# A fourth column buffer, paced prefetches and held loads around the down projection of a transformer-block training step

## The chip, the cores and the metric

The kernel runs on one core of one Trainium2 chip. The metric is the device time of one execution in microseconds (us); lower is better. A time quoted for a kernel is the median of its runs. Runs of one kernel spread by 0.4 to 0.8%, so every comparison is made by ratio against the kernel before, run in the same rounds on the same chip, with a 95% interval.

## The reference

The program computes a pre-layernorm block, linear attention followed by a SwiGLU feed-forward net, and then all its gradients. S = 2048 tokens, D = 640, F = 1728, 32 heads, bfloat16.

```python
h  = x + attention(layernorm(x), wqkv, wo)          # linear attention, phi = elu+1
h2 = h + (silu(n @ w_gate) * (n @ w_up)) @ w_down   # n = layernorm(h)
return h2, and the gradients of x, wqkv, wo, w_gate, w_up, w_down for grad_out
```

## The kernel before

The token axis is cut into ST = 16 tiles of 128 rows. The parts that matter come in this order:

- Phase A builds a mask `Mbd` (which elements belong to the same head) by small matmuls, and uses it in phase A and again in phase D.
- The feed-forward stage makes m, dg and du (features by tokens) and stores them in device memory. Its last matmuls are `accw` (weight gradients), whose results are stored from `dw_sb`.
- The down projection (`accf`) reads one column block `mcols` of m per tile. Between its tiles the gate and up weights are transposed on TensorE (`pt_w`).
- The dh1 stage (`acch`) reads `dgcols` and `ducols` per tile. During it, three big tensors for phase D (`oTr`, `rdenTr`, `pqTr`) are prefetched in 12 pieces of 640 KB.

A scheduler places each engine's instructions. Program order is its guide, not its result, so loads may be issued earlier than the text of the kernel suggests.

```python
    Mbd = const.tile([P, DT, D], BF16, name="Mbd")      # held for the whole kernel
# ... phase A
        for i in range(DT):
            for (n0, n1) in NCH:
                ps = psA.tile([P, 512], FP32, name="ps_mbd", tag="mm")
                nc.tensor.matmul(ps[:, :n1 - n0], lhsT=Efull[:, i * P:(i + 1) * P], rhs=Efull[:, n0:n1], start=True, stop=True)
                nc.vector.tensor_copy(out=Mbd[:, i, n0:n1], in_=ps[:, :n1 - n0])
# ... after the feed-forward stage (whose dw_sb, dwd_sb buffers come from a pool "dwo", bufs=2)
            wgT = wTp.tile([P, FT, D], BF16, name="wgT")
            wuT = wTp.tile([P, FT, D], BF16, name="wuT")
            if fsz[-1] < P:
                nc.any.memset(wgT[fsz[-1]:, FT - 1, :], 0.0)
                nc.any.memset(wuT[fsz[-1]:, FT - 1, :], 0.0)
            stream4 = pb4.enter_context(tc.tile_pool(name="stream4", bufs=3))
            stream = pwd.enter_context(tc.tile_pool(name="stream", bufs=3))
            # ...
            def load_cols(t):
                dgcols = stream4.tile([P, FT, P], BF16, name="dgcols")
                ducols = stream4.tile([P, FT, P], BF16, name="ducols")
                for (cols, scr_vv, eng) in ((dgcols, scr_dgT_v, nc.sync), (ducols, scr_duT_v, nc.scalar)):
                    eng.dma_start(out=cols[:, :, :], in_=scr_vv[:, :, t * P:(t + 1) * P])
                return dgcols, ducols
            # ... down projection
            for t in range(ST):
                if t == ST - 1:
                    for te in range(min(2, ST)):
                        early_cols[te] = load_cols(te)
                mcols = stream.tile([P, FT, P], BF16, name="mcols")
                nc.sync.dma_start(out=mcols[:, :, :], in_=scr_mT_v[:, :, t * P:(t + 1) * P])
                # ... 2 x 14 matmuls accf, h2t = accf + h1, store h2t
                if t < len(wblocks):
                    weight_rowblock_T(*wblocks[t], t)        # 14 transposes pt_w
            # ... dh1 stage
            for t in range(ST):
                for (dst_ap, src_ap) in pf_at.get(t, []):    # one of 12 pieces per tile, by the program's text
                    nc.gpsimd.dma_start(out=dst_ap, in_=src_ap)
                # ... dgcols, ducols = early or load_cols(t); 2 x 28 matmuls acch
                ln_bwd_tile(accs, hn_tm[:, t, :], rstd2[:, t:t + 1], dh2_tm[:, t, :], dh1_tm[:, t, :], workL)
```

## Time and profile before

The time is 1116.3 us (1113.9 to 1118.1, five runs). The profiled execution spans 1117.2 us.

| what | us | where to read it |
|---|---|---|
| TensorE busy | 1056.8 (95%) | busy table of the page |
| TensorE waits for the fourth tile's dgcols | 11.2 | waits of PE |
| TensorE waits for the first mcols | 4.1 | waits of PE |
| last accw matmul issued to first accf | 7.1 | timeline (607.75 to 614.86) |
| dh1 stage, first to last acch | 135.2 | timeline (687.12 to 822.36) |

The first view is the list of TensorE's waits in the kernel before: who waited, for whom, then microseconds in total, number of times, longest. Lines are left out at each `...`; the largest entry of all, 13.6 us for `xn_tm` (10.9 of it before TensorE's first matmul), is among them, and the change does not touch it.

```profile
...
PE acch L663 <- DMA dgcols<-scr_dgT: 11.2, 1, 11.2
PE accf L621 <- DMA mcols<-scr_mT: 4.1, 1, 4.1
PE pt_tr L127 <- ACT o_tm L91: 3.7, 3, 2.8
...
PE accw L561 <- ACT dw_sb L91: 2.9, 1, 2.9
...
PE ps_mbd L323 <- DVE Mbd L324: 1.0, 3, 0.4
...
```

The second view is the chain that ended last in the kernel before, in order of time: start, length, what the chain went through.

```profile
608.13 6.69 DMA mcols<-scr_mT
614.86 14.19 PE accf L621 x84
...
687.12 5.88 PE acch L663 x42
693.02 28.23 DMA dgcols<-scr_dgT
721.30 101.37 PE acch L663 x728
```

A load whose median is 3.9 us took 28.2 us. The timeline of POOL, the engine that issues the prefetch, suggests why (start, length, engine, line, what, and in brackets the idle time before it):

```profile
690.42 3.48 POOL L651 DMA_DIRECT2D oTr<-scr_oT  x4 [2.52 <-issue]
693.90 3.43 POOL L651 DMA_DIRECT2D rdenTr<-scr_rdenT  x4
697.32 1.72 POOL L651 DMA_DIRECT2D pqTr<-scr_pqT  x2
699.88 0.86 POOL L651 DMA_DIRECT2D pqTr<-scr_pqT  x1 [0.85 <-DMA oTr<-scr_oT]
702.14 0.87 POOL L651 DMA_DIRECT2D pqTr<-scr_pqT  x1 [1.40 <-DMA oTr<-scr_oT]
```

The text asks for one piece per tile, but nothing holds a piece back. All 12, 7.9 MB, are issued within 12 us. The view by stretches of time gives busy time of each engine, the granted TensorE clock, the DMA share and GB/s for the dh1 stage of the kernel before:

```profile
core 0: us, PE busy (x) PEld busy (x) DVE busy (x) ACT busy (x) POOL busy (x), PEclk, DMA share, GB/s
686.00:695.00 9.00, 8.42 (x63) 5.93 (x62) 0.49 (x1) 0.71 (x3) 5.12 (x7) 1.00 0.38 115
695.00:720.00 25.00, 15.10 (x112) 10.66 (x109) 7.11 (x19) 4.11 (x12) 5.76 (x7) 0.85 1.07 325
720.00:730.00 10.00, 8.70 (x48) 5.55 (x49) 1.77 (x2) 1.35 (x3) 0.00 (x0) 0.70 1.04 166
730.00:822.00 92.00, 92.00 (x680) 66.28 (x678) 35.53 (x84) 22.62 (x60) 0.00 (x0) 1.00 0.45 101
```

The DMA engines are full from 695 to 720, TensorE loses about 10 of those 25 us, and the granted clock is low afterwards (0.70 in 720 to 730). From 730 on, with the prefetch over, TensorE is never idle.

### The profile page before, as it was taken

Reading aid. Unit: us, or ns where it says so; the run is one execution under the profiler, and the core shown is the slowest. Engines: PE = TensorE matmul, PEld = TensorE weight load, DVE = VectorE, ACT = ScalarE, POOL = GpSimd, SP = SyncE. Lnnn points to the kernel's source line nnn. Section 1 sums busy time; section 2 is a strip of 40 time slices with the busy share of each in tenths; the row PEclk is TensorE's granted clock in tenths of the full one; section 3 lists DMA queues with packets and bytes.
Section 4 is the critical chain, followed back from the end, with each engine's and each line's share of the span. In section 5 each row is a group of like instructions: output and inputs, shape, how many; then the busy total and the mean of one; then the engine's idle time right before and its main releaser. Section 6 shows DMA issues by size and latency. Waiting matters only on the chain.

```text
span 1117.2 us, 20344 instructions
## 1 busy us (share of the span) xinstructions
PE 1056.8 (95%) x8297; PEld 716.7 (64%) x8337; DVE 572.1 (51%) x1441; ACT 483.4 (43%) x951; POOL 133.8 (12%) x224
## 2 busy tenths in 40 slices
PE   5899998999999999999997999599989999899998
PEld 2477664575847576666756677377767467577775
DVE  8766676727273545545361232234343985477321
ACT  6755586526262535345351010122233686744231
POOL 2100000120202111111312013000000000011110
PEclk9899898999999999999999899799999999999999
DMA  8234364312222222212045954955440039411100
GB/s 318 81 132 161 147 248 145 124 62 86 92 82 95 78 102 78 97 45 104 31 165 175 219 127 143 299 116 127 100 152 32 1 115 358 177 42 43 42 36 31
DMA packets 134669, 134.24 MB, mean 120 GB/s; under 512 B 92384, under 2 KB 115680, under 8 KB 134320
## 3 DMA queue, kind: packets, MB, share of 16 engines
q0 software_dynamic: 20208, 77.58, 18.7%
q1 hardware_dynamic: 85440, 48.03, 15.3%
q10 hardware_dynamic: 28928, 7.34, 3.3%
q8 instruction: 65, 1.06, 0.4%
q14 instruction: 28, 0.23, 0.1%
HBM read 71.50 MB, written 61.42 MB: 119 GB/s over the span
## 4 chain that ended last, share of the span: by engine, by line
PE 78%; DVE 8%; DMA 7%; ACT 5%; issue 2%; POOLq 0%; POOL 0%; ACTq 0%; DVEq 0%; SPq 0%
PE accw L561 10%; PE acch L663 10%; PE acc_dxn L837 6%; PE accf L621 6%; PE acc_dwqkv L856 6%; PE pu L498 5%; PE pg L494 4%; PE acc L552 4%; PE pt_trs L127 4%; PE pt_tr L127 4%; PE pdm L502 3%; DMA dgcols<-scr_dgT 3%; PE ps_k L336 2%; PE acc_dwo L697 2%; PE ps_v L341 2%; PE ps_do L721 2%
## 5 line engine op out<-in xcount | busy, mean ns | idle before, releaser
L561 PEld LDWEIGHTS <-hn_tm 128*128 128x128 bf16 x1120 | 108.6, 99 | 15.4 <-issue 4.0
L663 PE MATMUL acch<-wgT,dgcols 128*128 128x320 bf16 x448 | 67.9, 304 | 11.8 <-DMA dgcols<-scr_dgT 11.2
L494 PE MATMUL pg<-hnT,wg_blk 128*128 128x512 bf16 (+1 forms) x266 | 72.7, 383 | 4.0 <-DMA wg_blk<-in_B_w_gate_dram 3.4
L498 PE MATMUL pu<-hnT,wu_blk 128*128 128x512 bf16 (+1 forms) x274 | 74.5, 384 | 0.4
L89 DVE CAST dw_sb<-accw 128x256 bf16<-128x256 f32 (+1 forms) x35 | 14.5, 415 | 112.5 <-PE accw L561 81.8
L502 PE MATMUL pdm<-dh2T,wdT 128*128 128x512 bf16 (+1 forms) x274 | 69.3, 379 | 1.4 <-ACT dm L511 1.0
L552 PE MATMUL acc<-dh_tm,m_strip 128*128 128x320 bf16 (+1 forms) x448 | 69.3, 299 | 0.0
L621 PE MATMUL accf<-wd_big,mcols 128*128 128x320 bf16 x448 | 65.0, 307 | 4.1 <-DMA mcols<-scr_mT 4.1
L663 PE MATMUL acch<-wuT,ducols 128*128 128x320 bf16 x448 | 66.6, 300 | 0.0
L856 PE MATMUL acc_dwqkv<-cur_tm,xn_tmr 128*128 128x320 bf16 x480 | 65.7, 299 | 0.0
L561 PE MATMUL accw<-dg_strip,hn_tm 128*128 128x256 bf16 (+1 forms) x560 | 62.0, 273 | 2.9 <-ACT dw_sb L91 2.9
L663 PEld LDWEIGHTS <-dgcols 128*128 128x128 bf16 x448 | 44.4, 99 | 30.1 <-DMA dgcols<-scr_dgT 11.5
L561 PE MATMUL accw<-du_strip,hn_tm 128*128 128x256 bf16 (+1 forms) x560 | 60.3, 269 | 0.6 <-DVE dw_sb L89 0.6
L621 PEld LDWEIGHTS <-mcols 128*128 128x128 bf16 x448 | 44.1, 100 | 22.6 <-DMA mcols<-scr_mT 4.2
L856 PEld LDWEIGHTS <-xn_tmr 128*128 128x128 bf16 x480 | 46.9, 98 | 18.1
L91 ACT CAST dw_sb<-accw 128x256 bf16<-128x256 f32 (+1 forms) x35 | 12.8, 365 | 104.6 <-PE accw L561 102.0
L214 ACT ACTIVATE lb_dy<-acch 128x320 bf16<-128x320 f32 x32 | 14.0, 437 | 98.1 <-PE acch L663 98.1
L663 PEld LDWEIGHTS <-ducols 128*128 128x128 bf16 x448 | 44.1, 98 | 17.5
L552 PEld LDWEIGHTS <-m_strip 128*128 128x128 bf16 (+1 forms) x448 | 41.8, 99 | 13.6 <-issue 0.3
L502 PEld LDWEIGHTS <-wdT 128*128 128x128 bf16 (+1 forms) x280 | 27.0, 98 | 34.5 <-DVE wdT L89 3.1
L229 DVE SCALAR_TENSOR_TENSOR lb_t<-lb_dy,lb_nm,lb_t 128x640 bf16<-128x640 bf16 x32 | 28.2, 881 | 40.6 <-ACT lb_t L227 40.6
L565 POOL DMA_DIRECT2D out_dram<-dw_sb x70 | 37.9, 541 | 80.2 <-DVE dw_sb L89 45.2
(264 smaller groups left out, 2066.9 us busy)
## 6 DMA issues: line engine op xcount, KB each, us to landing
scr_mT<-mT_row POOLq DMA_DIRECT2D x14, 512.0 KB, 3.0
scr_duT<-duT_row POOLq DMA_DIRECT2D x14, 512.0 KB, 3.7
scr_dgT<-dgT_row POOLq DMA_DIRECT2D x14, 512.0 KB, 2.9
ducols<-scr_duT ACTq DMA_DIRECT2D x16, 448.0 KB, 4.6
mcols<-scr_mT SPq DMA_DIRECT2D x16, 448.0 KB, 4.1
dgcols<-scr_dgT SPq DMA_DIRECT2D x16, 448.0 KB, 3.9
out_dram<-dw_sb POOLq DMA_DIRECT2D x60, 64.0 KB, 1.8
x_tm<-in_A_x_dram SPq DMA_DIRECT2D x4, 640.0 KB, 6.2
```

The lines of the kernel that those rows point to most:

```text
L127: nc.tensor.transpose(out=pt[:cols_in, j * rows_in:(j + 1) * rows_in], in_=src, identity=ident[:rows_in, :rows_in])
L229: nc.vector.scalar_tensor_tensor(out=t2[:], in0=dy[:], scalar=nm[:, 0:1], in1=t1[:], op0=ALU.subtract, op1=ALU.subtract)
L494: nc.tensor.matmul(pg[:fs, :], lhsT=wg_blk[:, kt, coff:coff + fs], rhs=hnT[:, kt, cs], start=(kt == 0), stop=(kt == DT - 1))
L498: nc.tensor.matmul(pu[:fs, :], lhsT=wu_blk[:, kt, coff:coff + fs], rhs=hnT[:, kt, cs], start=(kt == 0), stop=(kt == DT - 1))
L502: nc.tensor.matmul(pdm[:fs, :], lhsT=wdT_i[:, kt, :], rhs=dh2T[:, kt, cs], start=(kt == 0), stop=(kt == DT - 1))
L552: nc.tensor.matmul(acc[:fs, :w], lhsT=m_strip[:, t, coff:coff + fs], rhs=dh2_tm[:, t, n0:n1], start=(t == 0), stop=(t == ST - 1))
L561: nc.tensor.matmul(acc[:, :gw], lhsT=hn_tm[:, t, dt_ * P:(dt_ + 1) * P], rhs=strip[:, t, :gw], start=(t == 0), stop=(t == ST - 1))
L565: nc.gpsimd.dma_start(out=o_ap[dt_ * P:(dt_ + 1) * P, gcol0:gcol0 + gw], in_=dw_sb[:, :gw])
L621: nc.tensor.matmul(acc[:, :w], lhsT=mcols[:, j, :], rhs=wd_nat[:, j, n0:n1], start=(j == 0), stop=(j == FT - 1))
L663: nc.tensor.matmul(acc[:, :w], lhsT=cols[:, j, :], rhs=wT[:, j, n0:n1], start=(k == 0), stop=(k == 2 * FT - 1))
L837: nc.tensor.matmul(acc[:, :w], lhsT=srcT[:, jj, t * P:(t + 1) * P], rhs=wqkvT[:, j, n0:n1], start=(k == 0), stop=(k == D3T - 1))
L856: nc.tensor.matmul(acc[:, :w], lhsT=xn_tmr[:, t, dt_ * P:(dt_ + 1) * P], rhs=cur_tm[:, t, n0:n1], start=(t == 0), stop=(t == ST - 1))
```

## The change

The intent is to remove both waits. `Mbd` no longer stays in the scratchpad for the whole kernel: it is built twice, which frees room for a fourth pair of column buffers. Each prefetch piece waits for the end of the tile before. The first four pairs of column loads wait until the down projection has started on the tile of the same number, so that the first mcols has no company. The first three mcols wait for the last accw matmul. The tile loops are also split into pairs (TB = 2). In the program's text this moves the first two pairs of column loads from before the last tile of the down projection to before the last two, and the change also puts each tile's column loads ahead of its prefetch piece.

```diff
-    Mbd = const.tile([P, DT, D], BF16, name="Mbd")
+    def build_mbd(Mbd_t, ps_pool, tag):
+        ...                                             # the same matmuls, evictions on either engine:
+                nc.any.tensor_copy(out=Mbd_t[:, i, n0:n1], in_=ps[:, :n1 - n0])
...
+        Mbd = kvA.tile([P, DT, D], BF16, name="Mbd")    # phase A
+        build_mbd(Mbd, psA, "mm")
...
-            stream4 = pb4.enter_context(tc.tile_pool(name="stream4", bufs=3))
+            stream4 = pb4.enter_context(tc.tile_pool(name="stream4", bufs=4))
...
-                    eng.dma_start(out=cols[:, :, :], in_=scr_vv[:, :, t * P:(t + 1) * P])
+                    d = eng.dma_start(out=cols[:, :, :], in_=scr_vv[:, :, tp * P:(tp + 1) * P])
+                    if tp < 4:
+                        tc.add_manual_dep(d.ins, down_mm[tp].name, SYNC, reason="first mcols tile goes alone")
...
+                    if t < 3:
+                        tc.add_manual_dep(dm_.ins, last_w.ins.name, SYNC, reason="not beside the dw_sb stores")
...
+                        d = nc.gpsimd.dma_start(out=dst_ap, in_=src_ap)
+                        tc.add_manual_dep(d.ins, tile_done[t - 1].name, SYNC, reason="one prefetch piece per tile")
...
+        Mbd = kvD.tile([P, DT, D], BF16, name="Mbd_d")  # phase D, again
+        build_mbd(Mbd, psD, "mm")
```

`down_mm[t]` is the first accf matmul of tile t, `last_w` the last accw matmul, `tile_done[t]` the last VectorE instruction of tile t of the dh1 stage.

More of the change, by code (lines that the diff above doesn't have):

```diff
@@ L13 @@
 AX = mybir.AxisListType
+SYNC = mybir.DependencyInfo(mybir.DependencyClass.Sync, mybir.DependencyReason.DATA)
 P = 128
@@ L117, in tiles_overlapping @@
         return [i for i in range(DT) if not (head_range(i)[1] <= c0 or head_range(i)[0] >= c1)]
+    def build_mbd(Mbd_t, ps_pool, tag):
+        for i in range(DT):
+            for (n0, n1) in NCH:
+                ps = ps_pool.tile([P, 512], FP32, name="ps_mbd", tag=tag)
+                nc.tensor.matmul(ps[:, :n1 - n0], lhsT=Efull[:, i * P:(i + 1) * P], rhs=Efull[:, n0:n1], start=True, stop=True)
+                nc.any.tensor_copy(out=Mbd_t[:, i, n0:n1], in_=ps[:, :n1 - n0])
     def transpose_into(dst_fn, src_fn, nblk, rows_in, ps_pool, tag="tr", cols_in=P, group=8, eng=None):
@@ L230, in ln_bwd_tile @@
                                        op0=ALU.subtract, op1=ALU.subtract)
-        nc.vector.scalar_tensor_tensor(out=dst_t, in0=t2[:], scalar=rstd_col, in1=resid_t, op0=ALU.mult, op1=ALU.add)
+        return nc.vector.scalar_tensor_tensor(out=dst_t, in0=t2[:], scalar=rstd_col, in1=resid_t, op0=ALU.mult, op1=ALU.add)
     def phi_from_psum(dst, ps, rows, cols, work):
@@ L318 @@
         nc.gpsimd.dma_start(out=scr_pqT_v, in_=pqT[:])
+        build_mbd(Mbd, psA, "mm")
         for i in range(DT):
-            for (n0, n1) in NCH:
-                ps = psA.tile([P, 512], FP32, name="ps_mbd", tag="mm")
-                nc.tensor.matmul(ps[:, :n1 - n0], lhsT=Efull[:, i * P:(i + 1) * P], rhs=Efull[:, n0:n1], start=True, stop=True)
-                nc.vector.tensor_copy(out=Mbd[:, i, n0:n1], in_=ps[:, :n1 - n0])
             pt = psT.tile([P, 8 * P], BF16, name="pt_et", tag="tr")
@@ L560 @@
                         for t in range(ST):
-                            nc.tensor.matmul(acc[:, :gw], lhsT=hn_tm[:, t, dt_ * P:(dt_ + 1) * P], rhs=strip[:, t, :gw],
-                                             start=(t == 0), stop=(t == ST - 1))
+                            last_w = nc.tensor.matmul(acc[:, :gw], lhsT=hn_tm[:, t, dt_ * P:(dt_ + 1) * P], rhs=strip[:, t, :gw],
+                                                      start=(t == 0), stop=(t == ST - 1))
                         dw_sb = dwo.tile([P, gwa], BF16, name="dw_sb")
@@ L580, with load_cols @@
             wd_nat = wd_big
-            def load_cols(t):
+            TB = 2 if ST % 2 == 0 else 1
+            down_mm = {}
+            def load_cols(tp):
                 dgcols = stream4.tile([P, FT, P], BF16, name="dgcols")
@@ L608 @@
             early_cols = {}
-            for t in range(ST):
-                if t == ST - 1:
-                    for te in range(min(2, ST)):
+            for tp in range(ST // TB):
+                if tp == ST // TB - 1:
+                    for te in range(2):
                         early_cols[te] = load_cols(te)
-                mcols = stream.tile([P, FT, P], BF16, name="mcols")
-                nc.sync.dma_start(out=mcols[:, :, :], in_=scr_mT_v[:, :, t * P:(t + 1) * P])
-                h2t = outp.tile([P, D], BF16, name="h2t")
-                accs = []
-                for ci, (n0, n1) in enumerate(NCH):
-                    w = n1 - n0
-                    acc = ps_f.tile([P, 512], FP32, name="accf")
-                    for j in range(FT):
-                        nc.tensor.matmul(acc[:, :w], lhsT=mcols[:, j, :], rhs=wd_nat[:, j, n0:n1],
-                                         start=(j == 0), stop=(j == FT - 1))
-                    accs.append(acc)
-                for ci, (n0, n1) in enumerate(NCH):
-                    nc.vector.tensor_tensor(out=h2t[:, n0:n1], in0=accs[ci][:, :n1 - n0],
-                                            in1=h1r[:, t, n0:n1], op=ALU.add)
-                nc.gpsimd.dma_start(out=o0_v[:, t, :], in_=h2t[:])
-                if t < len(wblocks):
-                    weight_rowblock_T(*wblocks[t], t)
@@ new lines @@
+                for tt in range(TB):
+                    t = tp * TB + tt
+                    mcols = stream.tile([P, FT, P], BF16, name="mcols")
+                    dm_ = nc.sync.dma_start(out=mcols[:, :, :], in_=scr_mT_v[:, :, t * P:(t + 1) * P])
+                    if t < 3:
+                        tc.add_manual_dep(dm_.ins, last_w.ins.name, SYNC, reason="not beside the dw_sb stores")
+                    h2t = outp.tile([P, D], BF16, name="h2t")
+                    accs = []
+                    for ci, (n0, n1) in enumerate(NCH):
+                        w = n1 - n0
+                        acc = ps_f.tile([P, 512], FP32, name="accf")
+                        for j in range(FT):
+                            mm = nc.tensor.matmul(acc[:, :w], lhsT=mcols[:, j, :], rhs=wd_nat[:, j, n0:n1],
+                                                  start=(j == 0), stop=(j == FT - 1))
+                            down_mm.setdefault(t, mm.ins)
+                        accs.append(acc)
+                    for ci, (n0, n1) in enumerate(NCH):
+                        nc.vector.tensor_tensor(out=h2t[:, n0:n1], in0=accs[ci][:, :n1 - n0],
+                                                in1=h1r[:, t, n0:n1], op=ALU.add)
+                    nc.gpsimd.dma_start(out=o0_v[:, t, :], in_=h2t[:])
+                    if t < len(wblocks):
+                        weight_rowblock_T(*wblocks[t], t)
@@ L645 @@
             pf_at = {}
+            tile_done = {}
             for k, piece in enumerate(pf_pieces):
@@ L648 @@
                 pf_at.setdefault(t_issue, []).append(piece)
-            for t in range(ST):
-                for (dst_ap, src_ap) in pf_at.get(t, []):
-                    nc.gpsimd.dma_start(out=dst_ap, in_=src_ap)
-                if t in early_cols:
-                    dgcols, ducols = early_cols.pop(t)
-                else:
-                    dgcols, ducols = load_cols(t)
-                accs = []
-                for ci, (n0, n1) in enumerate(NCH):
-                    w = n1 - n0
-                    acc = ps_h.tile([P, 512], FP32, name="acch")
-                    k = 0
-                    for (cols, wT) in ((dgcols, wgT), (ducols, wuT)):
-                        for j in range(FT):
-                            nc.tensor.matmul(acc[:, :w], lhsT=cols[:, j, :], rhs=wT[:, j, n0:n1],
-                                             start=(k == 0), stop=(k == 2 * FT - 1))
-                            k += 1
-                    accs.append(acc[:, :w])
-                ln_bwd_tile(accs, hn_tm[:, t, :], rstd2[:, t:t + 1], dh2_tm[:, t, :], dh1_tm[:, t, :], workL)
+            for tp in range(ST // TB):
+                for tt in range(TB):
+                    t = tp * TB + tt
+                    if t in early_cols:
+                        dgcols, ducols = early_cols.pop(t)
+                    else:
+                        dgcols, ducols = load_cols(t)
+                    for (dst_ap, src_ap) in pf_at.get(t, []):
+                        d = nc.gpsimd.dma_start(out=dst_ap, in_=src_ap)
+                        tc.add_manual_dep(d.ins, tile_done[t - 1].name, SYNC, reason="one prefetch piece per tile")
+                    accs = []
+                    for ci, (n0, n1) in enumerate(NCH):
+                        w = n1 - n0
+                        acc = ps_h.tile([P, 512], FP32, name="acch")
+                        k = 0
+                        for (cols, wT) in ((dgcols, wgT), (ducols, wuT)):
+                            for j in range(FT):
+                                nc.tensor.matmul(acc[:, :w], lhsT=cols[:, j, :], rhs=wT[:, j, n0:n1],
+                                                 start=(k == 0), stop=(k == 2 * FT - 1))
+                                k += 1
+                        accs.append(acc[:, :w])
+                    tile_done[t] = ln_bwd_tile(accs, hn_tm[:, t, :], rstd2[:, t:t + 1], dh2_tm[:, t, :], dh1_tm[:, t, :], workL).ins
```

## The prediction

> **What bounds the kernel.** TensorE: the page's busy table gives PE 1056.8 us of 1117.2 (95%), and the chain of waits puts 78% of the span on PE. The change aims at the two largest PE waits (view of PE's waits):
>
> - C: in the stage that makes dh1 (acch), PE stands still for 11.2 us until the fourth tile's dgcols lands. The chain shows that load under way for 28.2 us (693.0 to 721.3), against a median of 3.9 us. In the timeline 12 prefetch pieces of 640 KB (oTr, rdenTr, pqTr) are issued back to back at 690.4 to 702.1; by windows, the DMA share is 1.0 to 1.1 at 325 GB/s from 695 to 720. Afterwards the granted clock is 0.50 and the next 28 matmuls take 6.1 us instead of 3.8: another 2.3 us.
> - B: at the start of the down projection PE waits 4.1 us for the first mcols, which takes 6.7 us because three ducols loads and two more mcols run beside it. At 0.50 clock (615 to 620), the first 84 matmuls then take 14.2 us instead of 11.4.
>
> The Trainium skill ("DMA: Bandwidth & Descriptors", Issuing engines are not separate DMA queues) says that all issuing engines share 16 DMA engines; C agrees. "TensorE: Matmul & The Clock Gate", Part 1, says that an idle PE falls to half clock; the 0.50 after both waits agrees.
>
> **What the change does.**
> 1. Mbd leaves the constants, its room becomes a fourth buffer for dgcols and ducols, and tiles 0 to 3 are loaded during the down projection. Prefetch pieces go one per tile. Per 7.6 us tile that is 896 + 640 KB, about 200 GB/s, under the 325 seen. C should vanish whole: -13.5 us. The stage then takes 16 x 7.6 = 122 us, not 135.4.
> 2. ducols wait for the first matmul of their tile, so the first mcols runs ahead of its own queue only: estimate about 4.1 us to landing. PE gets 18 more weight transposes before the first accf, whose start their evictions then set: estimate 613.0 instead of 614.9. Gain 1.9 us, 1.4 us for transposes done early, and about 2 of the 2.8 us of slow clock, since gaps stay short: -5 us.
> 3. The wait of mcols for the last accw matmul changes nothing: before, too, issues them at 608.1, when it ends.
> 4. Building Mbd in phase A with evictions on both engines: PE waited 1.0 us on DVE there: -0.8 us.
> 5. Building it again in phase D: 10 matmuls, 5 evictions on each of ACT and DVE (0.43 and 0.48 us), where both are busy with o_tm and PE already idles 3.7 us (823 to 834): +2 us.
>
> Pairing the tiles (TB) only splits a loop. All of 1, 2 and 4 lies on the chain; 5 mostly.
>
> **Predicted:** 1116.3 - 13.5 - 5 - 0.8 + 2 = 1099 us; 1094.5 to 1106, 8 times in 10. Faster by over 2% (below 1094.0): 0.09; within 2%: 0.90; slower: 0.01.
>
> **What would show it.** No wait of PE on dgcols over 1 us, and no 0.50 clock in that stage; the prefetch pieces spread over some 90 us with landings well under 18 us; first mcols landing near 4 us; first accf about 2 us earlier after the last accw.
>
> **What would make it wrong.** Evictions of the early transposes delaying accf; cols loads slowed by each piece, so that dgcols is late again; phase D losing over 4 us to Mbd evictions.

## The result

The changed kernel takes 1100.1 us (1096.7 to 1100.9, eight runs) where the kernel before takes 1116.8 (15 runs in all). The ratio is 0.9845, with a 95% interval of 0.9831 to 0.9859: about 17 us. A ratio is the mean time of one kernel's fast runs over that of the other's fast runs of the same rounds, so it is not quite the ratio of the medians. In later rounds the same kernel gave 0.9859.

TensorE's waits in the changed kernel:

```profile
...
PE accw L566 <- ACT dw_sb L92: 2.8, 1, 2.8
...
PE accf L636 <- DMA mcols<-scr_mT: 2.1, 2, 1.6
PE accf L636 <- DVE h2t L641: 1.8, 1, 1.8
PE pt_tr L134 <- ACT o_tm L92: 1.4, 2, 1.2
...
PE ps_mbd L123 <- DVE Mbd L124: 0.4, 1, 0.4
...
```

The 11.2 us wait for dgcols is gone, and so is the 4.1 us wait for the first mcols. In their place smaller waits of accf stand inside the down projection, 3.9 us together. The POOL timeline of the changed kernel shows the prefetch paced by the dh1 tiles:

```profile
698.19 0.89 POOL L674 DMA_DIRECT2D oTr<-scr_oT  x1 [14.58 <-issue]
703.04 0.89 POOL L674 DMA_DIRECT2D oTr<-scr_oT  x1 [3.96 <-DVE dh_tm L238]
710.70 0.86 POOL L674 DMA_DIRECT2D oTr<-scr_oT  x1 [6.77 <-DVE dh_tm L238]
718.30 0.87 POOL L674 DMA_DIRECT2D oTr<-scr_oT  x1 [6.75 <-DVE dh_tm L238]
```

The view by stretches of the dh1 stage in the changed kernel has the same first three lengths as the one of before: TensorE never stops after the first microsecond, the clock stays at 1.00, and the prefetch is spread over the stage.

```profile
682.00:691.00 9.00, 8.42 (x63) 5.93 (x62) 0.49 (x1) 1.01 (x4) 0.54 (x1) 1.00 0.16 44
691.00:716.00 25.00, 25.00 (x187) 18.01 (x185) 10.07 (x26) 6.49 (x18) 2.63 (x3) 1.00 0.82 193
716.00:726.00 10.00, 10.00 (x75) 7.21 (x74) 4.73 (x9) 2.58 (x8) 0.87 (x1) 1.00 1.07 215
726.00:804.00 78.00, 78.00 (x577) 56.17 (x575) 29.61 (x70) 18.85 (x50) 6.90 (x8) 1.00 0.70 151
```

The chain through the down projection of the changed kernel shows where the new waits come from:

```profile
610.36 3.82 PE accf L636 x28
614.18 0.02 issue
614.21 0.50 DVE h2t L641
614.71 0.28 issue
614.99 7.51 DMA out_dram<-h2t
...
622.62 0.19 DVE h2t L641
622.82 12.35 DMA mcols<-scr_mT
635.16 0.04 issue
635.21 3.98 PE accf L636 x28
```

A store of h2t takes 7.5 us and a load of mcols 12.3 us. The eight held column loads (448 KB each, all of them issued between 610.5 and 636.5) come down on these transfers.

The stages of both traces, by the start of the first and last matmul of each kind (differences are taken before rounding). The last column is the second profile of the changed kernel, from later rounds; it shows how much of a difference is chance.

| stage | before | changed | difference | changed, again |
|---|---|---|---|---|
| last ps_q to first ps_k (builds Mbd) | 4.9 | 3.4 | -1.4 | 3.1 |
| start to last accw, all told | 607.7 | 605.3 | -2.5 | 605.8 |
| last accw to first accf | 7.1 | 4.9 | -2.2 | 4.9 |
| first accf to first acch | 72.3 | 72.6 | +0.4 | 72.6 |
| dh1 stage, first to last acch | 135.2 | 121.6 | -13.7 | 121.6 |
| last acch to first ps_do (builds Mbd again) | 38.6 | 37.2 | -1.3 | 38.5 |
| first ps_do to last matmul | 250.7 | 250.3 | -0.4 | 252.6 |

The two traces differ by 19.5 us, more than the 17 us of the times: the profiled execution of the kernel before was one of its slower ones (1118.9 us).

### The profile page after: what moved, and what is told of

Read it like the earlier page. It is cut to its first block, busy times and chain, and to the rows that moved or that the text cites. A ratio compares the mean times of both kernels' runs of the same rounds, so it can differ in the third digit from the quotient of the medians.

```text
span 1097.7 us, 20376 instructions
## 1 busy us (share of the span) xinstructions
PE 1051.0 (96%) x8307; PEld 714.5 (65%) x8347; DVE 572.3 (52%) x1440; ACT 487.0 (44%) x962; POOL 133.9 (12%) x224
## 4 chain that ended last, share of the span: by engine, by line
PE 80%; DVE 8%; ACT 5%; DMA 4%; issue 2%; POOLq 0%; POOL 0%; DVEq 0%; ACTq 0%
PE acch L683 11%; PE accw L566 10%; PE acc_dxn L859 6%; PE acc_dwqkv L878 6%; PE pu L503 5%; PE pg L499 5%; PE pt_tr L134 4%; PE acc L557 4%; PE accf L636 4%; PE pt_trs L134 4%; PE pdm L507 3%; PE ps_k L341 2%; PE ps_v L346 2%; PE acc_dwo L719 2%; PE ps_do L743 2%
## 5 line engine op out<-in xcount | busy, mean ns | idle before, releaser
L636 PE MATMUL accf<-wd_big,mcols 128*128 128x320 bf16 x448 | 62.4, 299 | 3.9 <-DMA mcols<-scr_mT 2.1
L516 ACT CAST dm<-pdm 128x512 bf16<-128x512 f32 (+1 forms) x56 | 33.1, 590 | 29.4 <-PE pdm L507 28.4
```

What stands on the lines that cost most here:

```text
L516: nc.scalar.copy(out=dm[:fs], in_=pdm[:fs])
L636: mm = nc.tensor.matmul(acc[:, :w], lhsT=mcols[:, j, :], rhs=wd_nat[:, j, n0:n1], start=(j == 0), stop=(j == FT - 1))
```

## The experiments

Three questions were left. Which part of the change removes the big stall, the pacing or the fourth buffer? Why did the start of the down projection give about 2 us instead of 5? What does Mbd's second build cost? Ten further kernels and the changed kernel again were run, all with correct results, each in five rounds against the kernel before.

| run | median us | ratio to before | 95% interval |
|---|---|---|---|
| changed kernel | 1100.1 | 0.9845 | 0.9831 to 0.9859 |
| changed kernel again | 1099.0 | 0.9859 | 0.9838 to 0.9880 |
| Mbd part only | 1117.3 | 0.9987 | 0.9969 to 1.0005 |
| pacing only | 1104.5 | 0.9881 | 0.9864 to 0.9898 |
| Mbd part and fourth buffer only | 1106.4 | 0.9906 | 0.9890 to 0.9923 |
| changed, column loads not held | 1101.9 | 0.9868 | 0.9844 to 0.9893 |
| changed, mcols not held | 1099.6 | 0.9845 | 0.9826 to 0.9864 |
| changed, no pacing | 1105.4 | 0.9896 | 0.9875 to 0.9917 |
| changed, column loads spread | 1095.6 | 0.9818 | 0.9795 to 0.9841 |
| spread, mcols free, four store buffers | 1093.7 | 0.9789 | 0.9769 to 0.9808 |
| changed, Mbd built twice in phase D | 1101.6 | 0.9870 | 0.9852 to 0.9888 |
| spread, free, four buffers, memsets late | 1092.4 | 0.9786 | 0.9767 to 0.9805 |

### Pacing only

The edit, on the kernel before:

```diff
-                    nc.gpsimd.dma_start(out=dst_ap, in_=src_ap)
+                    d = nc.gpsimd.dma_start(out=dst_ap, in_=src_ap)
+                    tc.add_manual_dep(d.ins, tile_done[t - 1].name, SYNC, reason="one prefetch piece per tile")
...
-                ln_bwd_tile(accs, ...)
+                tile_done[t] = ln_bwd_tile(accs, ...).ins
```

Expected:

> The kernel before with only the pacing: each prefetch piece waits for the end of the tile before. Three column buffers, Mbd as before. Theory: the stall on dgcols came from the burst of twelve pieces, so pacing alone takes it away: 13 us faster than before, no PE wait on dgcols over 1 us. Rival: the fourth buffer is what covers the late load; then pacing alone with three buffers leaves a wait on dgcols of several us and gains less than 8 us.

Measured: ratio 0.9881, which is 13.3 us of 1117.5. No wait for dgcols is left in TensorE's list, and the dh1 stage takes 121.6 us, as in the changed kernel. The order of instructions on every engine is that of before (40 records of TensorE's matmuls are missing from the trace of before). The view by stretches, over nearly the whole dh1 stage of this run:

```profile
core 0: us, PE busy (x) PEld busy (x) DVE busy (x) ACT busy (x) POOL busy (x), PEclk, DMA share, GB/s
686.00:806.00 120.00, 120.00 (x886) 86.45 (x884) 44.38 (x105) 28.91 (x77) 10.40 (x12) 1.00 0.78 167
```

Pacing alone, with three buffers, wins the whole stall; the rival falls.

### Mbd part and fourth buffer, no pacing

```diff
 # the kernel before, with the Mbd part of the change and
-            stream4 = pb4.enter_context(tc.tile_pool(name="stream4", bufs=3))
+            stream4 = pb4.enter_context(tc.tile_pool(name="stream4", bufs=4))
```

> The kernel before with the Mbd part and the fourth column buffer, but no pacing and no new dependency. Theory (the burst makes the stall; a fourth buffer only buys one tile, 7.6 us): PE waits 3 to 5 us on dgcols or ducols of the fifth tile instead of 11.2 us on the fourth, so about 7 us of the stall are won, with Mbd's 3 us some 10 us faster than before. Rival (the fourth buffer is enough by itself): no wait over 1 us in that stage and 16 us faster than before.

Measured: ratio 0.9906, 10.5 us faster, with a wait of 4.3 us for dgcols, and 127.7 us for the dh1 stage. The theory holds and the rival falls: the fourth buffer buys one tile against a load that takes 28 us or more beside the burst. This run showed one more thing that was not expected: the mcols were issued at 583.9, long before the last accw matmul (605.0), and the gap between accw and accf was 0.1 us.

### The changed kernel without pacing

```diff
-                        tc.add_manual_dep(d.ins, tile_done[t - 1].name, SYNC, reason="one prefetch piece per tile")
```

> The changed kernel without the pacing of the prefetch pieces (same order of instructions on TensorE). Theory: the burst comes back and costs what one buffer less than 28 us covers: PE waits 3 to 5 us on the fifth tile's dgcols, plus some slow clock, so 4 to 7 us slower than the changed kernel, about 1105. Rival (the fourth buffer makes the pacing needless): 1100.

Measured: 1105.4 us, 0.9896 against 0.9845, about 5.7 us slower than the changed kernel (0.0051 of 1117.2; the two were not in the same rounds). The chain through the dh1 stage in the profile of this run, asked for up to 730 us, shows the burst back:

```profile
680.55 5.88 PE acch L682 x42
...
686.45 28.93 DMA dgcols<-scr_dgT
...
715.42 14.65 PE acch L682 x96
```

TensorE's wait was 4.3 us. The two runs together settle it: without pacing, the fourth buffer wins some 7 of the 11 us; with pacing it is not needed for this.

### The changed kernel without the hold on the column loads

```diff
-                    if tp < 4:
-                        tc.add_manual_dep(d.ins, down_mm[tp].name, SYNC, reason="first mcols tile goes alone")
```

> The changed kernel without the dependency that holds the first four pairs of column loads until the down projection runs. Theory from the traces (what the free start gives, about 2.2 us of wait and 2.6 us of slow clock, is paid back by PE waits of 3.9 us when the eight held loads come down together on the mcols and h2t transfers): the time stays within 2 us of the changed kernel, 1099 to 1102. Rival (the dependency is worth the 5 us that the prediction gave it): 1105.

Measured: 1101.9 us, with single runs from 1099.2 to 1107.7, so by time this is inconclusive between the two theories: by the ratios the hold is worth 1.0 to 2.6 us. The one profile shows more, last accw to first acch in 81.9 us (6.0 and 76.0) where the changed kernel takes 77.6, and 6.5 us of waits for mcols, but it is of the slowest of the six runs (1107.7 us), so these 4 us are not what the hold is worth in general. The hold also sets TensorE's order: without it 28 weight transposes stand before the first accf, as in the kernel before, and with it 46. Whether my theory that it gives almost nothing was too strong stays open; what it gives over the kernel *before* (79.4 us for the same stretch) is small.

### The column loads spread over the down projection

```diff
-                        tc.add_manual_dep(d.ins, down_mm[tp].name, SYNC, reason="first mcols tile goes alone")
+                        tc.add_manual_dep(d.ins, down_mm[2 + 4 * tp - (tp == 3)].name, SYNC, reason="one pair of cols per four tiles")
```

The order of instructions on TensorE, VectorE and POOL is exactly that of the changed kernel; only the moments of eight loads move, and with them their places on the two engines that issue them.

> The changed kernel with the four held pairs of column loads released by the first matmul of down-projection tiles 2, 6, 10 and 13 instead of 0, 1, 2 and 3; TensorE has the same order of instructions. Theory (the term of the prediction that came out too large, 5 us forecast against about 2, was eaten by these eight loads coming down together within four tiles): the PE waits of 3.9 us inside the down projection go below 1 us and the kernel takes 1096 to 1097.5. Rival (the waits there have another cause, such as the two h2t buffers or the loads of mcols themselves): waits stay at 3 us or more and the time at 1100.

Measured: 1095.6 us, ratio 0.9818, a little better than forecast. TensorE's waits between the last accw and the first acch are now these, and no wait of accf is among them:

```profile
PE pt_w L610 <- DVE wgT L90: 0.8, 2, 0.5
PE acch L683 <- DVE h2t L641: 0.6, 1, 0.6
PE pt_w L610 <- ACT wgT L92: 0.5, 1, 0.5
```

First accf to first acch takes 68.5 us instead of 72.6. The h2t buffers and the mcols loads were left alone, so the rival falls: the waits came from the bunched column loads.

### The changed kernel without the hold on mcols

```diff
-                    if t < 3:
-                        tc.add_manual_dep(dm_.ins, last_w.ins.name, SYNC, reason="not beside the dw_sb stores")
```

> The changed kernel without the dependency that holds the first three mcols loads until the last accw matmul. The prediction called this dependency idle, because before issues the loads then anyway; but with four column buffers the mcols buffers lie on other memory, free earlier, and the run with the fourth buffer alone issued them early. Theory: without it the first mcols land before accw ends, the accf start loses its 4.7 us gap to the last accw matmul, but the stores of dw_sb get slower and PE waits about 3 us for a dw_sb buffer (3.1 us in the run with the fourth buffer alone); the sum moves by less than 2 us, 1098 to 1102. Rival (the dependency is idle, as predicted): the same trace as the changed kernel, no early loads. Second rival (early loading is simply better): 1096 or less.

Measured: 1099.6 us, ratio 0.9845, the same as with the hold. The trace is not the same: the mcols are issued at 586.3 instead of 605.6, accf follows accw after 0.1 us (the scheduler now puts no weight transposes between them), and accw pays for it. TensorE's waits in this stretch:

```profile
PE accw L566 <- DVE dw_sb L90: 3.1, 2, 1.9
PE accw L566 <- ACT dw_sb L92: 3.0, 1, 3.0
PE accf L634 <- DMA mcols<-scr_mT: 0.8, 1, 0.8
```

Two stores of dw_sb beside the early loads, issued at 591.6 and 592.2, take 4.5 and 4.2 us here, against 1.8 in the changed kernel, and only two buffers are there to wait in. So the hold is not idle, as the prediction had it: it exchanges one wait for others, and the time does not tell the two apart.

### Spread loads, free mcols, four store buffers

```diff
 # on the kernel with spread column loads: the hold on mcols removed, and
-            dwo = pb2.enter_context(tc.tile_pool(name="dwo", bufs=2))
+            dwo = pb2.enter_context(tc.tile_pool(name="dwo", bufs=4))
```

> The previous kernel (column loads spread) with no dependency on the first mcols and with four instead of two buffers for the gradient tiles that are stored (dw_sb, dwd_sb). Theory: the only price of the early mcols is the wait of the dw_sb evictions for a free buffer; with four buffers that wait is gone, accf starts within 1 us of the last accw matmul, and the kernel takes 1091 to 1094. Rival (early mcols loads cost elsewhere too, by the DMA engines that they share): 1096 or more.

Measured: 1093.7 us, ratio 0.9789, in the theory's range. The wait on DVE's dw_sb is gone, the gap from accw to accf is 0.1 us. TensorE's order between accw and accf changed as in the run before. The early mcols had no other price that the time shows.

### The same, with the memsets late

```diff
-                nc.any.memset(wgT[fsz[-1]:, FT - 1, :], 0.0)
-                nc.any.memset(wuT[fsz[-1]:, FT - 1, :], 0.0)
+                for wT_ in (wgT, wuT):
+                    ms_ = nc.any.memset(wT_[fsz[-1]:, FT - 1, :], 0.0)
+                    tc.add_manual_dep(ms_.ins, last_w.ins.name, SYNC, reason="not ahead of the dw_sb evictions")
```

> The version with spread column loads, free mcols and four store buffers (1093.7 us), and the two memsets of the tails of wgT and wuT held until the last accw matmul. Theory: in all kernels so far the 2.8 us wait of accw on ACT comes from the memset of wuT that stands before the dw_sb eviction on ACT and waits for a store of the last rows; without it that wait and its slow clock (1.7 us) go: 1089 to 1091. Rival (ps_acc or the stores hold accw anyway): 1093 to 1095.

Measured: 1092.4 us (1087.4 to 1092.8), ratio 0.9786. The trace does what the theory says: no accw wait is left, and the last accw matmul starts at 598.2 instead of 602.4. It is the trace of the fastest of the five runs, and both memsets moved, so the share of each is not known. The times do not resolve the gain: the ratio of the version before is 0.9789, from other rounds, and the median missed the theory's range by 1.4 us. This version has the lowest ratio of all: about 0.7% faster than the changed kernel beside it on the same chip (0.9786 over 0.9859).

### Mbd part only

```diff
 # the kernel before, with Mbd built in phase A (evictions on either engine) and again in phase D; nothing else
```

> The kernel before with only the Mbd part of the change: Mbd is built in the first phase with evictions on either engine, not kept, and built again in the last phase. Three column buffers, no new dependency, no pacing. Theory from the two traces (Mbd's move is a gain, 2.0 us at the start and 1.6 us in phase D): 3 to 4 us faster than before. Rival, as the prediction had it (0.8 us gained, 2 us paid): 1 us slower than before. The stalls on dgcols (11.2 us) and mcols (4.1 us) stay in both.

Measured: ratio 0.9987 (0.9969 to 1.0005), 1.5 us faster with 2 us either way. That is between the two; it speaks against the rival's slowdown of 1 us, while a gain of 3 us is still inside the interval. Its profile is not used for lengths. From the other profiles: the stretch that builds Mbd in phase A is 4.9 us in both profiles with the old build, and 3.1 to 3.6 us in all others, so a gain of 1.3 to 1.8 us there is solid.

### Mbd built twice in phase D

```diff
         build_mbd(Mbd, psD, "mm")
+        Mbd_x = kvD.tile([P, DT, D], BF16, name="Mbd_x")     # read by nothing
+        build_mbd(Mbd_x, psD, "mm")
```

> The changed kernel with the second build of Mbd done twice (into a tile that nothing reads): ten more matmuls and ten more evictions at the start of phase D. The prediction charged 2 us for one build; the trace of the changed kernel showed none of it. Theory (the build fills time in which TensorE waits for o_tm evictions anyway): the time from the last acch matmul to the first ps_do matmul, 37.2 us in the changed kernel, grows by less than 1 us, and the whole by no more. Rival (a build costs about 2 us, and the changed kernel's phase D was short by luck or by another order): it grows by 2 us or more.

Measured: ratio 0.9870 against 0.9859 of the changed kernel beside it, and 39.6 us from the last acch to the first ps_do. The scheduler also reordered the start of phase D, so this is not one build more and nothing else. Against the 37.2 and 38.5 us of the two profiles of the changed kernel, the growth is 1.1 to 2.4 us: inconclusive between the theory and the rival for the *second* build. For the first build the profiles are clearer. The stretch takes 38.6 and 39.4 us without a build (before, pacing only) and 36.9 to 38.7 us with one (nine profiles). One build costs nothing that these profiles can show.

### The changed kernel again

No edit.

> The changed kernel itself again, so that the two kernels beside it are compared with it on one chip: 1098 to 1102, ratio to before 0.983 to 0.986.

Measured: 1099.0 us, ratio 0.9859, as expected. Its profile, beside the first one of the same program, shows where part of the spread between runs comes from. In both, TensorE waits for the weights wqkvT before `acc_dxn`, and then this happens. First execution, stretches around the wait:

```profile
953.00:956.00 3.00, 2.70 (x20) 1.95 (x20) 0.00 (x0) 0.47 (x2) 0.00 (x0) 1.00 1.02 362
956.00:959.00 3.00, 3.00 (x25) 2.15 (x22) 0.87 (x4) 0.59 (x3) 0.00 (x0) 1.00 0.89 313
```

Second execution, the same place:

```profile
955.50:958.00 2.50, 2.27 (x14) 1.51 (x14) 0.00 (x0) 0.00 (x0) 0.00 (x0) 0.81 1.02 365
958.00:961.00 3.00, 3.00 (x15) 1.78 (x14) 0.00 (x0) 0.53 (x2) 0.00 (x0) 0.59 0.91 321
```

The wait was 2.35 us in the first and 2.72 us in the second. The clock stayed at 1.00 in the first and fell to 0.59 on average over these 3 us in the second, and that stage (first to last acc_dxn) took 65.1 and 66.7 us. Differences of under 2 us in one pair of profiles are therefore not evidence.

## Why the prediction was right, point by point

The time was forecast at 1099 us and came out at 1100.1. Part of that is luck: errors that cancelled. The signs that the prediction named did come: no wait on dgcols, no slow clock in the dh1 stage, prefetch pieces issued from 698 to 779 us and landing within 6.2 us, and the first mcols landed 4.4 us after its issue.

1. *"C should vanish whole: -13.5 us."* Right. The dh1 stage went from 135.2 to 121.6 us, and the pacing alone gave 13.3 us. The rate I had estimated for the paced stage, about 200 GB/s, was met (193 and 215 GB/s in the view by stretches). But I credited the fourth buffer along with the pacing. The runs show that the pacing did it.
2. *"-5 us"* at the start of the down projection. Wrong in size: the stretch from the last accw to the first acch shrank by 1.8 us (79.4 to 77.6; pacing only, which leaves it as before, has 78.8, and the other profiles with both holds as in the change have 77.4 to 77.7). What I had listed came: accf started 2.2 us sooner after accw, and the first 84 accf matmuls took 11.6 us instead of 14.2 because the clock stayed at full speed. The transposes done early do not have to be done later, but their 1.4 us were not measured alone. The term that I left out is that eight held loads have to come down somewhere. They came down in the first tiles of the down projection, and TensorE paid 3.9 us in waits for h2t and mcols. The run with spread loads shows it: the same order on TensorE, no such waits, and a gain of 6.0 us (79.4 to 73.4) where 5 were forecast.
3. *"The wait of mcols for the last accw matmul changes nothing."* Wrong. In the kernel before the mcols are issued at 608.1, but in the changed kernel, freed of the hold, at 586.3. The fourth column buffer makes the difference: the kernels with the Mbd part alone and with the fourth buffer added differ in nothing else, and the first issues its mcols 0.4 us after the last accw matmul starts, as before does, the second 21 us before. From the tile sizes, the fourth column buffer pushes the mcols buffers 7,168 bytes per partition further on, past the strip that accw is still reading; this explanation is worked out from the code, while the issue times are measured. The time did not depend on it (ratio 0.9845 with and without), so the error had no effect on the sum.
4. *"-0.8 us"* in phase A. Right in kind, too small: about 1.5 us, because the gaps there had also cost clock (0.82 in 45 to 53 us before, 1.00 after).
5. *"+2 us"* in phase D. Wrong: no cost is visible. I added the evictions' time to engines that looked full. The trace of the changed kernel shows TensorE waiting 1.4 us for o_tm evictions instead of 3.7: the scheduler, given the new work, also moved a 1.39 us memset on VectorE from before the o_tm evictions to behind them. That the move of the memset is the cause was not tested alone.

The sum of what was measured is 13.7 + 1.8 + 1.5 + 0 = 17.0 us, against 16.7 by the medians. Forecast was 17.3: the 3 us too many in point 2 were offset by the nearly 3 us too few in points 4 and 5.

Of the skill's statements used: "DMA: Bandwidth & Descriptors", Issuing engines are not separate DMA queues, agrees with the runs. POOL's prefetch slowed SP's loads from 3.9 to 28 us, and beside a paced piece the same loads still take about 6.3 us, which the 7.6 us tile hides. The half clock after an idle TensorE ("TensorE: Matmul & The Clock Gate", Part 1) agrees too: 0.50 was granted after the 11.2 us wait.

## What to carry to other kernels

A prefetch that is written one piece per tile is not paced unless each piece waits for something in its tile; look at the issue times on its queue, and pace it before buying buffers for the loads that it delays. When loads are held back to clear the way for an urgent one, ask when they will all be released: here they took back 3.9 us a few tiles later, and spreading them gave 4 us more by the traces, and 3 to 4.6 us by the times. A dependency that seems idle can start to matter when a buffer is added elsewhere.

## What the Trainium skill lacked or had wrong

- "TensorE: Matmul & The Clock Gate", Why this matters for your kernels, advises no idle gaps of TensorE over about 3 us. Here shorter ones cost clock as well: after 2.83 us the next 3 us ran at 0.50 (the dw_sb wait of the changed kernel), after 2.72 us the clock fell to 0.59, while 2.35 us at the same place in another execution left it at 1.00. Nor does length alone decide: at the same place a wait of 3.09 us left the clock at 1.00 in the last run (memsets late). The page's free-running window of Part 1, 3413 ns, fits: in all the traces the granted clock changes only on a grid of 3.41 us. Put on this grid, the 2.72 us wait left one step 61% idle, and the 3.09 us wait left two steps 45% and 46% idle. Part 1 asks for at least one idle window; here a step that was 61% idle was enough.
- "DMA: Bandwidth & Descriptors", Why small descriptors are slow (HBM only), explains the loss but gives no measured trn2 rate for loads of 256-byte rows. Here the column and mcols loads, 448 KB each in 256-byte rows, with some stores beside them, moved 218 to 223 GB/s with the DMA engines full (DMA share 1.36 to 1.39, 611 to 620 us of the changed kernel), against 325 GB/s in the prefetch burst.
- No page says what a small-row load suffers beside a large-row one. The same page, Queues, rings and completion order, says that each engine serves queue rows in turn, packet by packet. Here a 448 KB load took 28.2 us beside 7.9 MB of prefetch with rows of 1 KB, close to the end of the whole burst. That the row size decides it was not tested.
